# Decay attention and sticky mixture of experts: batch 0's first four heads of q and k turned in fp32 by TensorE, other places in SyncE's queue, another earliest time for gate products

## The chip, the cores and the metric

The kernel runs on one core of one Trainium2 chip. The metric is device time in microseconds (us) of one execution, lower is better. The kernel before takes 856.01 us, the median of 3 runs (855.11 to 859.09).

Engines are named as in the profile: PE (TensorE matmul) and PEld (its weight loads), ACT (ScalarE), DVE (VectorE), POOL (GpSimd), SP (SyncE, which here only issues DMAs, in order). "L868" is line 868 of the kernel before.

## The reference

Attention over 8 batches and 8 heads with 576 positions and a head size of 64, with a decay that is a running sum of logarithms, then a routing of every token to one of 8 experts, which a second gate may keep at the token before.

```python
# q, k, v: 8 x 8 x 576 x 64 fp32, f: 8 x 8 x 576
scores = np.matmul(q, k.transpose(0, 1, 3, 2)) / np.sqrt(D)
cum = np.cumsum(np.log(np.clip(f, 0.0001, 1.0)), axis=-1)
scores = np.where(causal, -1e9, scores + cum[..., :, None] - cum[..., None, :])
attn = softmax(scores)
x = np.matmul(attn, v)                     # tokens: 8 x 576 x 512
logits, local = x @ w_gate, sigmoid(x @ w_local)
# expert of token s: argmax(logits) if s == 0 or local < 0.5, else that of token s - 1
out = p[e] * (np.maximum(x @ w1[e], 0) @ w2[e])   # w1: 8 x 512 x 1024, w2: 8 x 1024 x 512
```

## The kernel before

**Precision.** fp32 numbers are split into two fp16 halves, a high one and the rest, so that matmuls run in fp16. Scores of a head are two matmul passes into one PSUM bank `st`: `Aq` with `Ak` (128 rows: the high and the low half of 64 elements), and `QB` with `KB` (70 rows: the high half again, 64 rows, and 6 rows of decay parts).

**Attention.** A batch is 25 units: per two heads five units of one 512 column bank (c, a, a, b, c), then four units for the last 64 rows (d) and one that joins them. A unit's stages are `sc` (scores on PE, L868, L875), `mx` (row maximum on DVE, L879), `ex` (exponent on ACT, L899, into `P`), `tr` (four fp32 transposes on PE, L914, into `pt`), `hi` and `lo` (the split into `ph` on ACT, L919, and `pl` on DVE, L923) and `av` (the product with v, L893). PSUM holds four banks `st`, two `pt`, two `xp`.

**The planner.** The order on every engine is fixed when the program is built. `issue` (L1221) holds a clock per engine, in ns, with fixed costs per stage, and always issues the stage that could start first by those clocks, with a weight per stage (W, RANK). Extra work is put in by due times (DUE: functions that run once the planned time is reached), by `turns` (PE transposes of the next batch's q and k, L457, with an eviction by ACT or DVE, L466 to L470), by `pump` (POOL's splits), by `ship` (loads on SP), and by a side chain: gate products (`mult`, L816) and the routing steps, mostly DVE operations. A `mult` reads `xt` and `xlt`, which are DMA transposes of the finished tokens `xr` (512 rows) and `xl` (the last 64 rows, L781); `side_next` (L1184) lets it go once the three transposes are issued (`XD`).

**Batch 0's q and k** have a path of their own (`start`, L576). Heads 0 to 3: ACT makes the high half in token layout (`high`, L521), POOL or DVE the low half (`low`), PE turns the halves with two kinds of fp16 matmul (`turn_first`, L546, into `pt`; `turn_high`, L552, into `st`) and adds the decay rows to the second (`add_decay`, L557), DVE and ACT move them to `Aq`, `Ak`, `QB`, `KB` (`untwist`, L561, L563). Heads 4 to 7 are split by POOL (`pieces`, L703 to L705), turned by DMA transposes (`turn`, L362, L365; L370 for the last 64 rows) and copied to QB and KB by DMA. The decay parts come from a chain on ACT and DVE: L228, L229 (logarithm), L231 (scan), then `by_chunks` and `parts` (L238 to L251), which fill `spk`, the operand of `add_decay`. The same `parts` makes `spt` for the last 64 positions.

**SyncE's queue.** SP issues DMAs in program order, and a DMA whose inputs are not ready holds all behind it. The loads of q and k of the batch after next (`load_main`, `load_last`, L162, L169), the copies of the next batch's high halves to QB and KB (`copy_hi`, `copy_last`, L375, L378, L382), the decay rows (L339, L341, L351) and the transposes L751 and L781 all go there. ORD0, ORDA and ORDB (L43 to L45) are lists of moves, two-part codes that `moves` (L621) turns into such issues and POOL steps for batches 0 to 2.

After attention come the experts: matmuls with weights that are loaded and split on the way (L1690, L1712).

Of the kernel before, what the change touches and what calls it, by code (L numbers as in the profile page):

```python
# [9 lines left out]
F32 = mybir.dt.float32  # L10
# [10 lines left out]
BIG = 32768.0  # L21
# [21 lines left out]
ORD0 = moves_of("q:l :k2 q:t4 k:l q:p k:t4 q0:m :sv k:p q:c k:c q1:m q:t k:t :lm q:M k:m :at 0:R 1:R :lv")  # L43
ORDA = moves_of("q0:P k:M 0:V 1:V k:ag")
ORDB = moves_of("q:ag q:G0 2:V q1:P k0:P k1:P q:e k:e 3:V q:G1 k:G0 :vl :Vl q:2 k:G1 :iv v0:P k:2")  # L45
# [20 lines left out]
DUE = (("k2", 11000), ("q2", 12500), ("k3", 14500), ("q3", 15500), ("v", 18000), ("v4", 20500), ("a", 26000), ("b", 29000))  # L66
# [6 lines left out]
def kernel(  # L73
# [38 lines left out]
    nc.gpsimd.memset(ident16, 0.0)  # L112
    nc.gpsimd.affine_select(out=ident16, in_=ident16, pattern=[[-1, 128]], compare_op=ALU.not_equal, fill=1.0, base=0,
                            channel_multiplier=1)
# [37 lines left out]
    mask(mB, 0.0, 2, [[-1, 2], [-2, 64]], 1, ALU.not_equal, BIG)  # L152
    mask(mA, 0.0, 2, [[1, 2], [2, 64]], -1, ALU.is_ge, -BIG)
# [74 lines left out]
    nc.vector.tensor_scalar(ft, ft, 1e-4, 1.0, ALU.max, ALU.min)  # L228
# [125 lines left out]
    def split_qk(b, nm, g0, g1, fast=False):  # L354
        t16, t = Tq[b][nm + "t"], LT[b, nm]
        hi, lo = (t16[:, :, 0:64], t16[:, :, 64:128]) if nm == "q" else (t16[:, :, 64:128], t16[:, :, 0:64])
        split(hi[:, g0:g1], lo[:, g0:g1], t[:, g0:g1], fast)

    def turn(b, nm, h0, h1):
        t16, A = Tq[b][nm + "t"], Tq[b][nm + "A"]  # L360
        if nm == "k":
            nc.sync.dma_start_transpose(out=A[:, 4 * h0:4 * h1], in_=flat(t16[:, 4 * h0:4 * h1]))  # L362
            return
        for c in range(2):
            nc.sync.dma_start_transpose(  # L365
                out=A[:, 16 * c + 2 * h0:16 * c + 2 * h1, :].rearrange("p a (r x) -> p (a r) x", r=2),
                in_=flat(t16[64 * c:64 * c + 64, 4 * h0:4 * h1]))
# [16 lines left out]
    def scale_q(b, g0, g1):  # L384
        t = LT[b, "q"][:, g0:g1]
        nc.scalar.mul(t, t, SCALE)

    def prep_qk(b, nm):

        def begin():  # L390
            new_prep(b, nm)
            prep_aug(b, nm)
            if nm == "q":
                scale_q(b, 0, 16)
                clock["ACT"] += 950

        def turns(h0):
            if nm == "q" and h0 == 0:
                scale_q(b, 16, 36)
                clock["ACT"] += 1150  # L400
            if nm == "k" and h0:
                turn(b, nm, h0, h0 + 5)
            else:
                turn(b, nm, h0, h0 + 4)
                if h0:
                    turn_last(b, nm)

        def half(g0, g1):
            R = {}

            def parts(i):
                t, t16 = LT[b, nm], Tq[b][nm + "t"]
                if not R:
                    hi, lo = (t16[:, :, 0:64], t16[:, :, 64:128]) if nm == "q" else (t16[:, :, 64:128], t16[:, :, 0:64])
                    R["p"] = hi_lo(hi[:, g0:g1], lo[:, g0:g1], t[:, g0:g1], (g1 - g0) // 2)
                R["p"][i][1]()

            return [(64 * (g1 - g0), lambda i=i: parts(i)) for i in range(3)]

        def copy(g0, g1):  # L420
            A, B = Tq[b][nm + "A"], Tq[b][nm + "B"]
            nc.sync.dma_start(out=B[0:64, g0:g1], in_=(A[0:64] if nm == "q" else A[64:128])[:, g0:g1])

        return ([(0, begin)] + half(0, 16) + [(0, lambda: turns(0))] + half(16, 36) + [(0, lambda: turns(4))],
                [(0, lambda: copy(0, 16)), (0, lambda: copy(16, 36))])

    turns = deque()

    def prep_turned(b, nm):
# [20 lines left out]
        def group(j):  # L450
            U = {}

            def tq():
                t16 = Tq[b][nm + "t"]
                U["pt"] = psS.tile([128, 8, 128], F16, name="st")
                for a in range(4 if j == 4 else 8):
                    nc.tensor.transpose(U["pt"][:, a], t16[:, 8 * j + a], ident16)  # L457

            def eq():
# [13 lines left out]
                elif j == 4:  # L473
                    copy_last(b, nm)
# [1792 lines left out]
```

## Time and profile before

| what | value |
|---|---|
| median of 3 runs | 856.01 us (855.11 to 859.09) |
| profiled execution, its own time | 858.83 us |
| its span in the trace | 857.1 us |
| mean granted TensorE clock | 0.976 |
| busy: PE, PEld | 785.4 us (92%), 546.9 us (64%) |
| busy: DVE, ACT, POOL | 529.3 us (62%), 434.4 us (51%), 408.9 us (48%) |

The table is one profiled execution. Busy is the time in which an engine ran something; its idle time is what the views of waits explain. The granted clock is a share of full speed: near 1.0 in a stretch is the level of 2.4 GHz, near 0.5 that of 1.2 GHz. The first score runs at 16 us, batch 1 begins at 70 us, and from about 460 us only experts run.

### The profile page before, as it was taken

The numbers are of one execution on the slowest core, as the hardware profiler recorded it, in microseconds if no ns is written. First come the engines' busy times: TensorE is split into PE (matmuls) and PEld (weight loads), VectorE is DVE, ScalarE is ACT, GpSimd is POOL, SyncE is SP. The second block draws the span as 40 slices with busy tenths as digits, with TensorE's granted clock in tenths as the row PEclk, the third lists the DMA queues.
The fourth block names the chain that finished last, engine by engine and source line by source line (L and its number), as shares of the span: only waits on it lengthen the run. The fifth ranks groups of instructions, "written<-read, shape, count | busy, mean of one in ns | idle before, by whom it ended". The sixth has DMA issues, their size and how long they took to land. (4 is left out here: it accounts for less than half of the span.)

```text
span 857.1 us, 21126 instructions
## 1 busy us (share of the span) xinstructions
PE 785.4 (92%) x8510; PEld 546.9 (64%) x8510; DVE 529.3 (62%) x1125; ACT 434.4 (51%) x807; POOL 408.9 (48%) x479
## 2 busy tenths in 40 slices
PE   5897999889998799878987899999999999999996
PEld 3676778767877678767753555575564847566543
DVE  8885878898867888798848742443163644525120
ACT  4785878758866688657821413333242423324221
POOL 9598938488753968532976252221311212130201
PEclk9998999999989999998999999999999999999999
DMA  7979768596781859329674641848264553736101
GB/s 167 192 165 193 160 112 168 123 180 144 140 197 42 157 140 158 70 47 229 161 165 185 194 142 50 216 147 203 95 171 149 155 182 121 193 116 185 51 0 47
DMA packets 196517, 122.46 MB, mean 143 GB/s; under 512 B 136220, under 2 KB 172318, under 8 KB 196396
## 3 DMA queue, kind: packets, MB, share of 16 engines
q1 hardware_dynamic: 190273, 101.68, 51.6%
q0 software_dynamic: 6144, 19.41, 7.0%
q8 instruction: 68, 1.11, 0.5%
q14 instruction: 32, 0.26, 0.1%
HBM read 72.41 MB, written 19.62 MB: 107 GB/s over the span
## 5 line engine op out<-in xcount | busy, mean ns | idle before, releaser
L1690 PE MATMUL z<-xT,wh 128*128 128x288 f16 (+4 forms) x960 | 182.3, 301 | 3.8 <-DVE hl L1671 3.8
L899 ACT ACTIVATE P<-st,nm 128x512 f32<-128x512 f32 (+3 forms) x288 | 152.4, 584 | 38.5 <-DVE nm L879 35.3
L879 DVE TENSOR_REDUCE nm<-st 128x1 f32<-128x512 f32 (+4 forms) x264 | 134.1, 542 | 23.2 <-PE st L875 16.8
L1671 DVE SCALAR_TENSOR_TENSOR hl<-z,hh 128x576 f16<-128x576 f32 (+5 forms) x80 | 53.0, 662 | 154.0 <-ACT hh L1670 153.8
L919 ACT CAST ph<-pt 128x512 f16<-128x512 f32 (+1 forms) x200 | 115.8, 583 | 50.1 <-PE pt L914 48.6
L914 PE MATMUL pt<-ident,P 128*128 128x128 f32 x784 | 124.7, 283 | 13.0 <-DVE pl L923 8.0
L923 DVE TENSOR_TENSOR pl<-pt,ph 128x512 f16<-128x512 f32 x168 | 111.6, 668 | 26.3 <-ACT ph L919 24.0
L1690 PEld LDWEIGHTS <-wh 128*128 128x128 f16 x960 | 93.2, 98 | 43.7 <-issue 4.9
L1690 PE MATMUL z<-xT,wl 128*128 128x288 f16 (+4 forms) x480 | 118.4, 301 | 0.0
L1712 PE MATMUL y<-uh,hh 128*128 128x512 f16 x288 | 109.9, 381 | 1.6 <-ACT o L1680 1.6
L1712 PE MATMUL y<-uh,hl 128*128 128x512 f16 x288 | 109.9, 382 | 0.0
L1712 PE MATMUL y<-ul,hh 128*128 128x512 f16 x288 | 109.7, 381 | 0.0
L1670 ACT ACTIVATE hh<-z 128x576 f16<-128x576 f32 (+5 forms) x80 | 46.0, 575 | 121.1 <-PE z L1690 121.0
L914 PEld LDWEIGHTS pt<-ident,P 128*128 128x128 f32 x784 | 85.8, 144 | 28.9 <-issue 7.5
L1712 PEld LDWEIGHTS <-hh 128*128 128x128 f16 x576 | 56.5, 98 | 70.4 <-issue 6.2
L1682 POOL DMA_INDIRECT out_dram<-o,ranki x26 | 27.3, 1051 | 149.0 <-ACT o L1680 115.8
L893 PE MATMUL xp<-VH,pl 128*128 128x65 f16 (+1 forms) x960 | 92.3, 195 | 4.3 <-DVE pl L923 4.3
L893 PE MATMUL xp<-VH,ph 128*128 128x65 f16 (+1 forms) x960 | 94.3, 198 | 0.9 <-ACT ph L919 0.9
L893 PE MATMUL xp<-VL,ph 128*128 128x65 f16 (+1 forms) x960 | 93.2, 196 | 0.0
L893 PEld LDWEIGHTS <-ph 128*128 128x128 f16 (+1 forms) x1920 | 85.0, 103 | 7.7 <-issue 2.5
L868 PE MATMUL st<-KB,QB 70*128 70x256 f16 (+4 forms) x448 | 80.1, 287 | 8.5 <-DMA KB<-Ak 7.1
L868 PE MATMUL st<-Ak,Aq 128*128 128x256 f16 (+4 forms) x448 | 80.7, 291 | 7.3 <-ACT P L899 7.1
(390 smaller groups left out, 1316.3 us busy)
## 6 DMA issues: line engine op xcount, KB each, us to landing
stg<-in_moe_w_dram SPq DMA_DIRECT2D x64, 512.0 KB
xs<-xr SPq DMA_DIRECT2D x16, 512.0 KB
ldq<-in_q_dram SPq DMA_DIRECT2D x14, 512.0 KB
ldk<-in_k_dram SPq DMA_DIRECT2D x14, 512.0 KB
ldv<-in_v_dram SPq DMA_DIRECT2D x28, 256.0 KB
QB<-Aq SPq DMA_DIRECT2D x15, 256.0 KB
KB<-Ak SPq DMA_DIRECT2D x15, 256.0 KB
ldv<-in_v_dram SPq DMA_DIRECT2D x20, 64.0 KB
```

The lines of the kernel that those rows point to most:

```text
L868: nc.tensor.matmul(st[p0:p0 + m, co:co + n], lhsT=queries(lq, kk, h, c), rhs=rhs, start=(ps == 0 and first and co == col), stop=(ps == 1), ...
L879: nc.vector.tensor_reduce(dst, src, axis=AX.X, op=ALU.max, negate=True)
L893: nc.tensor.matmul(xo, lhsT=a[:, c0:c0 + m], rhs=w[:, vi, :], start=False, stop=(i == n - 1 and jj == 2), skip_group_check=True)
L899: nc.scalar.activation(P[:, c0:c1].rearrange("p (k x r) -> p k r x", r=2, x=64), st[:, c0:c1].rearrange("p (k r x) -> p k r x", r=2, x=64) ...
L914: nc.tensor.matmul(U["pt"][:, i * 128:(i + 1) * 128], lhsT=P[:, i * 128:(i + 1) * 128], rhs=ident, is_transpose=True, start=(i == 0), stop ...
L919: nc.scalar.copy(U["ph"][:, :cols], U["pt"][:, :cols])
L923: nc.vector.tensor_tensor(U["pl"][:, :cols], U["pt"][:, :cols], U["ph"][:, :cols], ALU.subtract)
L1670: nc.scalar.activation(hv, z[:, 0:nh, 0:wd], AF.Relu)
L1671: nc.vector.scalar_tensor_tensor(lv, z[:, 0:nh, 0:wd], 0.0, hv, ALU.max, ALU.subtract)
L1682: nc.gpsimd.indirect_dma_start(out=outf, out_offset=bass.IndirectOffsetOnAxis(ap=scat(t), axis=0), in_=o, in_offset=None, bounds_check=NT ...
L1690: nc.tensor.matmul(z[:, a, 0:wd], lhsT=w[:, d, fc * 128:(fc + 1) * 128], rhs=xT[:, x, a * wd:(a + 1) * wd], start=(i == 0), stop=(i == len ...
L1712: nc.tensor.matmul(y, lhsT=a[:, fc, t * 128:(t + 1) * 128], rhs=u[:, fc], start=(i == 0), stop=(i == len(prods) - 1))
```

## The change

Batch 0's heads 0 to 3 are turned by PE in fp32, straight from the loaded q and k, each head's four blocks into one bank (`turn_head`); after `add_decay` ACT reads the bank twice, for the high half in Aq or Ak (`head_hi`) and for QB or KB (`head_b`), and DVE makes the low half from the bank and the high half (`head_lo`). Heads 4 to 7 and the last 64 rows are still split by POOL, and are then turned by PE as in later batches (`group`, the former inner function of `prep_turned`), with evictions by ACT or DVE; the DMA transposes of q and k are gone. The planner gets these turns as entries with a ready time (LATE), and batch 0's later units need them. The factor on q moves into the evictions; the decay constants in `pick` make up for it.

Of the small work, `spk` and KB's ones are set by DVE and QB's by ACT (one ACT table load more); `spt` is made by POOL (`last_parts`); v's heads 2 to 7 of batch 0 are split by POOL, where ACT and DVE took heads 2 to 5; some masks come later. In SP's queue the loads of q and k for heads 4 to 7 stand ahead of v and of the decay parts, and the lists ORD0 to ORDC put batch 0's to 2's loads and copies in another order. A `mult` may not start by the planner before `XR`, 4.5 us behind the issue of the last rows' transpose.

```diff
-ORDB = moves_of("q:ag q:G0 2:V q1:P k0:P k1:P q:e k:e 3:V q:G1 k:G0 :vl :Vl q:2 k:G1 :iv v0:P k:2")
+ORDB = moves_of("q:ag q:G0 2:V q1:P k0:P k1:P 3:V q:G1 k:G0 :vl :Vl k:G1 :iv v0:P")
+ORDC = moves_of("q:2"), moves_of("k:2")
...
+XL = 4500
+LATE = ((12500, 'kh'), (13500, 'qh'), (15500, 'q2'), (15500, 'q3'), (17500, 'k2'), (17500, 'k3'), (22000, 'q4'), (23000, 'k4'))
...
+    for c in range(2):
+        nc.scalar.activation(flat(QB[0][64:70, 16 * c + 8:16 * c + 16]), ident[64:70, 0:1].broadcast_to([6, 1024]), AF.Copy,
+                             scale=0.0, bias=-1.0)
...
+    def turn_head(h, nm):
+
+        st = psX.tile([128, 512], F32, name="xp") if h == 2 else psS.tile([128, 512], F32, name="st")
         for a in range(4):
+            nc.tensor.matmul(st[0:64, 128 * a:128 * a + 128], lhsT=LT[0, nm][:, 4 * h + a], rhs=ident, is_transpose=True,
                              start=(a == 0), stop=True, skip_group_check=True)
         return st
...
+    def head_hi(st, h, nm):
+        nc.scalar.activation(of_head(Tq[0][nm + "A"], TOP if nm == "q" else LOW, h, nm), of_bank(st, 64, nm), AF.Copy,
+                             scale=SCALE if nm == "q" else 1.0)
+
+    def head_b(st, h, nm):
+        nc.scalar.activation(of_head(Tq[0][nm + "B"], slice(0, 70), h, nm), of_bank(st, 70, nm), AF.Copy,
+                             scale=SCALE if nm == "q" else 1.0)
...
+        for h in range(2):
+            heads(h)
+            for nm in "kq":
+                head_hi(HS[h, nm], h, nm)
+        decays(0)
+        decays(1)
+        heads(2)
+        decays(2)
+        for h in range(2):
+            for nm in "kq":
+                head_b(HS[h, nm], h, nm)
+                head_lo(HS[h, nm], h, nm)
         load_v(0, groups=((2, 8),), last=False)
+        vh, vl, v0 = parts_v(0, 2)
+        nc.scalar.copy(vh, v0)
+        for x in pieces("q", 4, 8):
+            x()
+        nc.gpsimd.tensor_tensor(vl, v0, vh, ALU.subtract)
...
             XD[b] = XD.get(b, 0) + 1
+            XR[b] = max(clock["POOL"], clock["PE"]) + XL
...
+        if hasattr(chain[0], "batch") and side["run"] is None:
+            after.append((XR[chain[0].batch], "PE"))
```

On SP, at the end of batch 0, the copies of batch 1's high halves (QB_121 and KB_123 before, QB_109 and KB_111 now, both from Aq and Ak) and the loads of batch 2's q and k stand like this. Before:

```order
L182 DMA ldv<-in_v_dram 128x8x64
L185 DMA ldv<-in_v_dram 64x4x64 x2
L162 DMA ldq<-in_q_dram 128x8x128 x2
L169 DMA ldq<-in_q_dram 64x4x64 x2
L162 DMA ldk<-in_k_dram 128x8x128 x2
L169 DMA ldk<-in_k_dram 64x4x64 x2
L378 DMA QB_121<-Aq 64x2x1024 x2
L382 DMA QB_121<-Aq 64x512
L375 DMA KB_123<-Ak 64x2048 x2
L382 DMA KB_123<-Ak 64x512
```

Now:

```order
L185 DMA ldv<-in_v_dram 64x4x64 x2
L362 DMA QB_109<-Aq 64x2x1024 x2
L366 DMA QB_109<-Aq 64x512
L162 DMA ldq<-in_q_dram 128x8x128 x2
L169 DMA ldq<-in_q_dram 64x4x64 x2
L359 DMA KB_111<-Ak 64x2048 x2
L366 DMA KB_111<-Ak 64x512
L162 DMA ldk<-in_k_dram 128x8x128 x2
L169 DMA ldk<-in_k_dram 64x4x64 x2
```

The copies to QB moved ahead of both loads, those to KB ahead of the load of k.

On SP, in batch 4, the transpose of batch 3's last rows (xlt) and the copies for batch 5, before:

```order
L757 DMA xs<-xr 64x4x1024 x2
L378 DMA QB_121<-Aq 64x2x1024 x2
L382 DMA QB_121<-Aq 64x512
L339 DMA KB_123<-augm 3x4096
L351 DMA KB_123<-augt 3x512
L781 DMA_TRANSPOSE xlt<-xl 128x4x128
L787 DMA xs<-xl 128x1x256 x2
```

Now:

```order
L732 DMA xs<-xr 64x4x1024 x2
L756 DMA_TRANSPOSE xlt<-xl 128x4x128
L763 DMA xs<-xl 128x1x256 x2
L362 DMA QB_109<-Aq 64x2x1024 x2
L366 DMA QB_109<-Aq 64x512
L341 DMA KB_111<-augm 3x4096
L353 DMA KB_111<-augt 3x512
```

The transpose moved ahead of four DMA groups; the same holds two batches later.

On DVE, at the third block of routing steps (HI, RH, LO), at the end of batch 6, before:

```order
L1473 TENSOR_TENSOR hm<-t_192,ov 128x10
L1479 TENSOR_TENSOR HI<-imain,hm 128x480
L1483 TENSOR_SCALAR RH<-HI,irow 128x10x48
L1485 TENSOR_SCALAR RH<-HI,irow 128x2x48
L1490 TENSOR_TENSOR RH<-HI,icol 128x10x48
L1491 TENSOR_TENSOR LO<-i_176,lo 128x1280
L879 TENSOR_REDUCE nm<-st 128x1 x5
```

Now:

```order
L855 TENSOR_REDUCE nm<-st 128x1 x2
L1451 TENSOR_TENSOR hm<-t_188,ov 128x10
L855 TENSOR_REDUCE nm<-st 128x1 x2
L1457 TENSOR_TENSOR HI<-imain,hm 128x480
L855 TENSOR_REDUCE nm<-st 128x2
L1461 TENSOR_SCALAR RH<-HI,irow 128x10x48
L899 TENSOR_TENSOR pl<-pt,ph 128x512
L1463 TENSOR_SCALAR RH<-HI,irow 128x2x48
L855 TENSOR_REDUCE nm<-st 128x1
L1468 TENSOR_TENSOR RH<-HI,icol 128x10x48
L1469 TENSOR_TENSOR LO<-i_172,lo 128x1280
```

The row maxima of the units that follow stand among the steps now, where they stood behind them.

## Rows read from the trace of the kernel before

**Rows 1.** What PE waited for, whole span (us in total, times, longest us).

```profile
PE st L868 <- DMA KB<-Ak: 7.1, 3, 4.5
PE st L868 <- ACT P L899: 7.1, 6, 4.7
PE st L816 <- DMA xlt<-xl: 4.4, 2, 2.4
PE st L868 <- DMA KB<-augt: 1.4, 1, 1.4
```

**Rows 2.** Busy time by engine in stretches around PE's long waits (stretch, its length, then each engine's busy us with its instructions, the granted TensorE clock, the DMA share and GB/s).

```profile
24.90:28.50 3.60, 3.60 (x20) 2.41 (x19) 1.77 (x4) 1.81 (x4) 1.69 (x2) 0.53 0.79 124
28.50:70.30 41.80, 38.02 (x590) 31.36 (x588) 35.09 (x74) 35.83 (x73) 33.39 (x44) 1.00 0.91 197
...
74.80:79.90 5.10, 5.10 (x73) 4.09 (x73) 2.89 (x6) 2.44 (x5) 3.17 (x3) 0.54 0.88 80
...
246.70:253.60 6.90, 6.86 (x43) 5.41 (x44) 3.44 (x11) 2.65 (x6) 0.68 (x2) 0.51 0.91 219
...
353.20:355.90 2.70, 2.70 (x19) 1.73 (x17) 2.13 (x7) 0.86 (x2) 2.45 (x5) 0.50 0.00 0
...
387.90:394.50 6.60, 6.58 (x48) 4.75 (x48) 4.46 (x14) 4.91 (x11) 0.00 (x0) 0.58 1.04 265
```

**Rows 3.** The end of batch 0 in order of time (start, length, engine, line, what, count, idle time before it and what ended it): SP's issues, and PE's second score pass of batch 1.

```profile
60.32 1.84 SPq L162 DMA_DIRECT2D ldk<-in_k_dram  x2
...
64.52 1.32 SPq L378 DMA_DIRECT2D QB<-Aq  x2
...
66.67 2.68 SPq L375 DMA_DIRECT2D KB<-Ak  x2
...
74.80 0.59 PE L868 MATMUL st<-KB,QB 70*128 70x512 f16 x1 [4.53 <-DMA KB<-Ak]
```

**Rows 4.** Size of one DMA of the loads of k (count, KB each), from the list of DMA issues up to 75 us, and the DMA rate (last column) in two stretches of the view by stretches.

```profile
ldk<-in_k_dram SPq DMA_DIRECT2D x4, 512.0 KB
...
60.00:65.00 5.00, 5.00 (x88) 4.32 (x87) 4.97 (x10) 4.06 (x10) 4.83 (x6) 1.00 1.19 274
...
70.00:75.00 5.00, 0.47 (x3) 0.20 (x2) 0.92 (x2) 0.37 (x1) 4.83 (x6) 0.76 1.17 184
```

**Rows 5.** The gate product of batch 3 in order of time: POOL's split of the last rows, SP's queue, and PE's wait; the last row is the same wait two batches later.

```profile
237.41 0.67 POOL L314 TENSOR_TENSOR xl<-xnl,xl 128x256 f16<-128x256 f32 x1
239.91 1.76 SPq L378 DMA_DIRECT2D QB<-Aq  x2
243.77 1.83 SPq L781 DMA_TRANSPOSE xlt<-xl  x1
246.74 0.59 PE L816 MATMUL st<-wg,xlt 128*64 128x18 f16 x8 [1.94 <-DMA xlt<-xl]
351.26 0.42 PE L816 MATMUL st<-wg,xlt 128*64 128x18 f16 x8 [2.42 <-DMA xlt<-xl]
```

**Rows 6.** The third block of routing steps in order of time: its last step on DVE, the row maxima behind it, and PE.

```profile
385.05 1.48 DVE L1491 TENSOR_TENSOR LO<-i,lo 128x1280 f16<-128x1280 f16 x1
386.45 3.32 DVE L879 TENSOR_REDUCE nm<-st 128x1 f32<-128x512 f32 x7
387.92 0.59 PE L868 MATMUL st<-Ak,Aq 128*128 128x512 f16 x1 [4.66 <-ACT P L899]
```

**Rows 7.** The start in order of time, all engines.

```profile
5.01 0.68 ACT L229 ACTIVATE lg<-ft 64x576 f32<-64x576 f32 x1 [2.93 <-DVE ft L228]
5.71 1.28 ACT L230 ACT_TABLE_LOAD   x1
7.00 0.20 ACT L230 ACTIVATE one<-one 1x1 f32<-1x1 f32 x1
11.30 0.78 DVE L246 CAST spk<-lg 4x512 f16<-4x512 f32 x1
12.13 1.01 PE L557 MATMUL st<-spk,pick 97*6 97x512 f16 x2 [0.74 <-DVE spk L246]
15.98 0.61 PE L868 MATMUL st<-Ak,Aq 128*128 128x512 f16 x1
16.57 2.20 POOL L705 TENSOR_TENSOR t16q<-ldq,t16q 128x1024 f16<-128x1024 f32 x1
16.82 2.00 DVE L247 CAST spt<-cu 64x64 f16<-64x64 f32 x1
18.66 0.41 PE L552 MATMUL st<-ident,t16k 128*64 128x128 f16 x4
21.41 0.38 PE L552 MATMUL st<-ident,t16k 128*64 128x128 f16 x4 [0.34 <-ACT QB L563]
24.28 0.38 PE L546 MATMUL pt<-ident,t16k 128*128 128x128 f16 x4 [2.17 <-DVE Ak L561]
26.93 1.06 PE L914 MATMUL pt<-ident,P 128*128 128x128 f32 x4
```

**Rows 8.** Durations up to 75 us by line and shape (count, busy us, mean ns), and a run of transposes from the view in order of time, at the full clock.

```profile
L466 ACT ACTIVATE Ak<-st 128x1024 f16<-128x1024 f16 x3 | 3.1, 1078 | 0.0
L563 ACT CAST QB<-st 70x512 f16<-70x512 f32 x4 | 2.3, 582 | 1.9 <-PE st L557 1.9
...
64.12 1.91 PE L457 MATMUL st<-ident,t16k 128*128 128x128 f16 x28
```

More of the change, by code (lines that the diff above doesn't have):

```diff
@@ L382, in copy_last @@
         nc.sync.dma_start(out=B[0:64, 32:36], in_=(A[0:64] if nm == "q" else A[64:128])[:, 32:36])
[L384 to L402, printed above, removed]
-            else:
[L404 to L425, printed above, removed]
@@ L513, in prep, with last_parts @@
         return q + [mark("q")] + k + [mark("k")] + v + last
+    def last_parts():
+        x = cu[:, 512:576]
+        for j in range(3):
+            nc.gpsimd.tensor_scalar(spt[:, j], x, 1.0, 1.0, ALU.mult, ALU.mult)
+            if j < 2:
+                nc.gpsimd.tensor_tensor(x, x, spt[:, j], ALU.subtract)
     def put_aug():
@@ L611, in start, with due_1, due_2 @@
         for x in ORD0:
+            moves(x)
+    def due_1():
+        assert all(n > -9 or u['key'][2] > 1 for n, u, _ in line['tq'])
+        for x in ORD1:
+            moves(x)
+    def due_2():
+        for x in ORD2:
             moves(x)
@@ L676, in moves @@
             u, i = b
[L677 to L683 removed]
+            for y in prep_v(1) if u == "v" else halves(1, u, *((0, 16), (16, 36))[int(i)]):
+                y[1]()
         else:
@@ L693, in due_b @@
     def due_b():
+        assert all(n > -9 for n, u, _ in line['tq'])
         for x in ORDB:
@@ L696, in due_b, with due_c @@
         open_small()
+        EX["run"] = True
+    def due_c(i):
+        for x in ORDC[i]:
+            moves(x)
     def pieces(nm, h0, h1):
@@ L730, in split_v, with decays @@
-    def split_v(h0, h1, fast=False):
-        tv = [x.rearrange("p (c h) d -> p c h d", c=4) for x in (VH[0][:, 0:32], VL[0][:, 0:32], LT[0, "v"][:, 0:32])]
-        split(tv[0][:, :, h0:h1, 0:64], tv[1][:, :, h0:h1, 0:64], tv[2][:, :, h0:h1], fast)
-    def due_v(h0, h1):
-        split_v(h0, h1, True)
-        clock["ACT"] += 480
-        clock["DVE"] += 600
-    XT, XD = {}, {}
+        for nm in "kq":
+            HS[h, nm] = turn_head(h, nm)
+    def decays(h):
+        for nm in "kq":
+            add_decay(HS[h, nm], h, nm)
@@ new lines, in due_head, with head_3, tq, eq @@
+    def due_head(nm):
+        head_hi(HS[2, nm], 2, nm)
+        head_b(HS[2, nm], 2, nm)
+        head_lo(HS[2, nm], 2, nm)
+        clock["ACT"] += 960
+        clock["DVE"] = max(clock["DVE"] + 640, clock["ACT"] + 800)
+    def head_3(nm):
+        U = {}
+        def tq():
+            U["st"] = turn_head(3, nm)
+            add_decay(U["st"], 3, nm)
+        def eq():
+            for f in head_hi, head_b, head_lo:
+                f(U["st"], 3, nm)
+            clock["DVE"] = max(clock["DVE"], clock["ACT"] + 1100) + 640
+        return {"key": (0, nm, -1), "tq": ("PE", 500, tq, {"psS": 1}, {}), "eq": ("ACT", 960, eq, {}, {"psS": 1})}
@@ L1773 @@
                 init_gate()
-            if not due:
+            if "run" in EX:
                 if b < B - 1 or i < XP:
```

251 lines of the change are left out of this document (97 added, 154 removed).

## Prediction

> **What bounds the kernel now.** I read PE's waits first, then busy time and granted clock around the long ones, then SP's queue and the start in order of time. PE is busy for 92% of the span, so time is to be had only where PE waits, or where it runs at the slow clock afterwards. The list of waits [rows 1] has four long single waits that this change can reach: 4.53 us for KB at the end of batch 0, 1.94 and 2.42 us for the last rows' transpose (xlt) in batches 4 and 6, and 4.66 us for a free bank at the end of batch 6. Behind each, the granted clock is near one half [rows 2]: 0.54 for 5.10 us, 0.51 for 6.90, 0.50 for 2.70, 0.58 for 6.60. PE is busy throughout these stretches, so a stretch of length t at clock c costs t x (1 - c): 2.3, 3.4, 1.35 and 2.8 us. The reader is to see that a wait costs about as much again behind it. From 460 us on only experts run, and nothing there is touched; a gain in attention is a gain at the end, since engine orders are fixed and serial.
>
> **The change part by part.** The sum is made against the profiled execution's own 858.83 us, which is 2.8 us above the median of 856.01.
>
> *End of batch 0.* The copies to KB are issued from 66.67 us, and PE gets the first one's data at 74.80 [rows 3]. They are 64 KB to 256 KB; what makes them late is what stands ahead in the queue: the loads of batch 2's q and k, of which those of k went out from 60.32. Two of these are 512 KB each, so k alone has 1.05 MB; at the rates of 274 and 184 GB/s of these microseconds [rows 4] that is 3.8 to 5.7 us of transfer. The order now has the KB copies ahead of the load of k, and the QB copies ahead of both loads. A transfer 3.8 to 5.7 us sooner covers a wait of 4.53, so I take it as gone, with the 2.3 us of slow clock: 6.8 us. Bounds: 0 (the load of q, still ahead, is enough to be late) to 6.8.
>
> *The gate products in batches 4 and 6.* POOL's split of the last rows is done at 238.08 (237.41 + 0.67), but SP issues the transpose at 243.77, because the QB copies of the next batch stand ahead, and these wait for evictions until 239.91 [rows 5]. PE then waits until 246.74. In the new order the transpose stands ahead of those copies in both batches, so it can go out some 5 us sooner, more than either wait. The products themselves stay at nearly the same place in PE's order. I take both waits and the slow stretches behind: 1.94 + 3.4 + 2.42 + 1.35 = 9.1 us. Bounds: 0 to 9.1. In batch 2 it is the other way round: the transpose now stands behind the copies, but the product comes some five units later, which is more than the 5 us lost.
>
> *End of batch 6.* DVE does the routing steps in one block to 386.53, and only then the seven row maxima for which ACT's exponents, and by them PE's banks, wait [rows 6]: 4.66 us and 2.8 behind. Now maxima stand between the steps. This comes out of the planner's arithmetic, not of an edit to the route, and DVE's work is the same; so I take half, 3.7 us, bounds 0 to 7.5.
>
> *The start.* (a) ACT has one more table load and two QB fills ahead of the logarithm. A load is 1.28 us [rows 7], a fill of 1024 columns about the 1.08 of the nearest row [rows 8]; together 3.4 us. ACT idles 2.93 us ahead of the logarithm, so 0.5 is left over: `spk` is complete at 12.08 + 0.5 = 12.6. (b) PE then has four decay products (two take 1.01), eight fp32 turns of head 2 (four fp32 transposes take 1.06 at this clock) and two decay products more before the first score: 2.0 + 2.1 + 1.0 = 5.1, so 17.7 instead of 15.98: 1.7 later. The turns of heads 0 and 1 need only loaded q and k and lie under the decay chain. (c) Head 2's turning, 18.66 to 21.41 before, is then behind: 2.75 back. (d) The 2.17 us for which PE waits at 24.28 are DVE's: its casts for `spt` lie beside POOL's long operations (16.82 for 2.00, POOL from 16.57 for 2.20). They are on POOL now, so that wait goes, and with it the slow stretch up to 28.5 at 0.53, 3.60 x 0.47 = 1.7 [rows 2]. (e) PE gets 40 fp16 turns of heads 4 to 7 and the last rows, which DMA did: 28 take 1.91 [rows 8], so 2.7 us. Head 3's turns are about equal. Sum: +1.7 - 2.75 - 2.17 - 1.7 + 2.7 = -2.2. Bounds: a chain whose cast meets a long POOL operation is held by up to 2.20 - 0.78 = 1.4, and without the gains of (d) this is +3.1 + 2.7 - 2.75 = +3.1; with the turns at the full clock (b) is half as long, and it is -4.8.
>
> The Trainium skill (ScalarE: Activation LUTs, "What ACT_TABLE_LOAD costs") gives 1283 ns for a load and about 1380 ns of drain, 2.66 us for a switch. The trace agrees with the first number only: the load ends at 6.99 and the next activation starts at 7.00 [rows 7]. By the page the logarithm, and all behind it, would be another 1.4 us later and the forecast 843.0; by the row nothing is added, and I go by the row.
>
> *What hides the rest.* New evictions (three of up to 1.08 on ACT, the others on DVE, one ACT cast of 0.58 more per head and operand) lie beside PE from 28.5 to 70.3, where ACT is busy 35.83 of 41.80 us and DVE 35.09 [rows 2]; two v casts leave ACT and three subtractions DVE. That cover is some 6 us; if it were gone, ACT's part is 2 x 1.08 + 0.6 + 4 x 0.58 less two v casts of about 0.6, near 4 us. The wait of 1.4 for the last rows' decay parts of KB [rows 1] goes, since their DMAs stand ahead of batch 1's v now: 1.4, bounds 0 to 1.4.
>
> *What the new order brings elsewhere.* Every later batch is planned anew, and waits like the four can arise where there were none. On average one of the four costs (4.53 + 1.94 + 2.42 + 4.66) / 4 = 3.4 and 2.5 behind, 5.9 us. I take one and a half of them, +8.8; bounds 0 and three, 17.7.
>
> Sum: -6.8 - 9.1 - 3.7 - 2.2 - 1.4 + 8.8 = -14.4: 844.4 for an execution like the profiled one, 841.6 for the median.
>
> **The rivals.** *The waits move.* The gate and routing terms (12.8 us) come back in other places and one more of 5.9 with them instead of one and a half: -10.4 + 5.9 = -4.5, 851.5. For it: these four waits are accidents of an order that the planner made with fixed costs, and it makes a new one with the same costs. Against it: the transposes of the last rows have moved for good, and the planner now counts 4.5 us for them.
>
> *The copies to KB stay late.* The load of q, as large as that of k, still stands ahead, and the evictions of k come last; the 6.8 do not come: 848.4. Against it: 1.05 MB less are ahead.
>
> *POOL is late in batch 0 (slower).* Place: the turns of the last rows of k, which stand in PE's order ahead of the second wave of scores. POOL has three splits of v more ahead of them (half of a 2.20 operation and its copy, some 1.7 us each, an estimate from [rows 7], so 5 us) and v's loads stand behind the decay parts in SP's queue. If POOL splits the last rows 5 us after PE is there, PE waits 5 and runs slow behind it for 2.5: with the waits moved as in the first rival, +7.5 - 4.5 = +3.0, and with ACT's cover gone as well +7.0, 863 for the median. It decides when PE's wait there passes some 12 us, or 5 where the gate terms fail too. Against it: POOL drops the low halves of heads 0 to 3 and q's scaling.
>
> *It does not do what it says.* The start may gain nothing, as the first score comes no sooner (17.7); with +3.1 for the start it is 846.9.
>
> **How the numbers follow.** Forecast 58%, own range 833 to 849; waits moved 17%; KB late 10%; start without gain 9%; slower 6%. Half a per cent, about what a measurement of this kernel tells from no change, is 4.3 us: faster means below 851.7. Of the waits moved, half lies below it; all of the forecast, KB late and the start count as faster but for 2 points: 58 + 10 + 9 + 8 - 2 = 83%. Same: 9 + 2 = 11%; slower 6%. The range of 8 in 10 is 830 to 853: below 830 all terms come at nearly their upper bounds with no new wait (-23.2), above 853 are the upper half of the waits moved and the slower case.
>
> **What would show it.** First score near 17.7 us and no wait of PE near 24; the wait for KB at the end of batch 0 below 1 us and the granted clock near 1.0 in the 5 us behind it; no wait of PE for xlt above 0.5 us; the first maxima of batch 7 before the last routing step. The prediction is wrong if the KB wait is still 4 us, if PE's waits in batches 2 to 7 have not fallen in sum, or if batch 1 begins later than the 70 us of now.

## The result and the profile after

The changed kernel takes 834.2 us, the median of 4 runs (832.92 to 835.73), against 856.55 for the kernel before on the same chip: ratio 0.9737, 95% interval 0.9705 to 0.9769, or 22.4 us less where 14.4 were forecast. The profiled execution takes 835.73 us, its span is 834.0.

To see where the gain lies, both spans are cut at the same three points of PE's work: the first mask product of the last rows' unit (L974 before, L950 after) of batches 0, 1 and 7. The first stage holds the start and most of batch 0, the second the step to batch 1, the third batches 2 to 6 with what overlaps them, the fourth the rest and the experts. The view of windows, kernel before (columns as in [rows 2]):

```profile
0.00:55.30 55.30, 39.54 (x458) 29.84 (x458) 46.23 (x83) 36.98 (x72) 43.94 (x70) 0.97 0.79 168
55.30:106.60 51.30, 45.01 (x699) 36.92 (x695) 37.90 (x80) 35.56 (x72) 46.21 (x79) 0.93 0.90 183
106.60:413.97 307.37, 278.22 (x4439) 226.56 (x4434) 252.96 (x604) 225.37 (x461) 192.06 (x211) 0.96 0.66 137
413.97:857.10 443.13, 422.63 (x2931) 253.59 (x2926) 192.25 (x359) 136.48 (x205) 126.66 (x122) 0.99 0.48 139
sum 857.10, PE 785.41 PEld 546.92 DVE 529.35 ACT 434.39 POOL 408.87; mean PE 196.35 PEld 136.73 DVE 132.34 ACT 108.60 POOL 102.22
```

The same view of the kernel after:

```profile
0.00:54.04 54.04, 42.58 (x519) 33.87 (x519) 42.45 (x89) 45.38 (x83) 39.04 (x69) 0.97 0.67 154
54.04:97.55 43.51, 40.38 (x650) 32.77 (x646) 35.44 (x75) 33.71 (x68) 41.69 (x51) 1.00 0.92 183
97.55:389.56 292.01, 269.63 (x4434) 221.75 (x4430) 252.73 (x604) 224.10 (x461) 197.54 (x240) 0.99 0.69 147
389.56:834.00 444.44, 424.12 (x2930) 254.09 (x2926) 193.49 (x359) 136.70 (x205) 126.55 (x121) 0.99 0.49 139
sum 834.00, PE 776.71 PEld 542.48 DVE 524.11 ACT 439.90 POOL 404.82; mean PE 194.18 PEld 135.62 DVE 131.03 ACT 109.97 POOL 101.20
```

The stages change by -1.26, -7.79, -15.36 and +1.31, in sum -23.1 us. PE's busy time falls by 8.7 us, but times the mean granted clock it is 785.41 x 0.976 = 767 before and 776.71 x 0.989 = 768 after. So PE's work is nearly the same, and the gain is 14.4 us of idle time and 8.7 us of slow clock.

PE's waits after (us in total, times, longest), against [rows 1]:

```profile
PE pt L890 <- DVE pl L899: 12.1, 15, 1.9
...
PE xp L869 <- DVE pl L899: 5.4, 7, 2.3
...
PE st L844 <- ACT P L875: 3.9, 9, 0.7
...
PE st L844 <- DMA KB<-Ak: 0.2, 1, 0.2
```

No wait for xlt is left, that for KB is 0.2 us in place of 7.1, and the one of 4.66 us of a score for a free bank has no successor above 0.7. The longest wait in batches 1 to 7 is 2.3 us.

The start after, in order of time on ACT, DVE and PE (answers to [rows 7]):

```profile
4.11 1.28 ACT L231 ACT_TABLE_LOAD   x1
5.40 0.68 ACT L231 ACTIVATE lg<-ft 64x576 f32<-64x576 f32 x1
...
6.32 1.06 PE L478 MATMUL st<-ident,ldq 128*64 128x128 f32 x4
...
9.46 0.28 DVE L251 COPY spk<-spm 4x512 f16<-4x512 f16 x1
9.76 0.68 DVE L253 TENSOR_TENSOR lg<-lg,spm 64x512 f32<-64x512 f32 x1
10.48 0.42 DVE L248 CAST spk<-lg 4x512 f16<-4x512 f32 x1
...
11.04 1.02 PE L483 MATMUL st<-spk,pick 97*6 97x512 f16 x4 [1.95 <-DVE spk L248]
11.99 0.63 PE L478 MATMUL xp<-ident,ldk 128*64 128x128 f32 x4
...
12.99 0.59 PE L483 MATMUL xp<-spk,pick 97*6 97x512 f16 x2
13.58 0.39 PE L844 MATMUL st<-Ak,Aq 128*128 128x512 f16 x1
```

The first score starts at 13.58 us, earlier than before (15.98) and not later, as forecast (17.7). The logarithm starts at 5.40, 0.39 later than before, as forecast; but the chain from there to `spk` is faster (its last cast takes 0.42 in place of 0.78), and PE is at full speed already: four decay products in 1.02 us, where two took 1.01. This is read from durations (four fp32 turns take 1.06 us at 6.32 and 0.63 at 11.99); the view of windows gives a granted clock of 1.00 for all of 5.50 to 13.58, and before for 8.96 to 15.98.

The gate product of batch 3, in order of time on POOL, SP and PE (answers to [rows 5]):

```profile
216.71 0.67 POOL L316 TENSOR_TENSOR xl<-xnl,xl 128x256 f16<-128x256 f32 x1
222.28 3.25 SPq L756 DMA_TRANSPOSE xlt<-xl  x1
...
228.54 0.42 PE L792 MATMUL st<-wg,xlt 128*64 128x18 f16 x8
```

The transpose stands ahead of the QB copies now, but it still goes out 4.9 us after POOL is done (217.38): SP is busy with issues of its own until then. What has moved is the product, 6.26 us behind the issue of the transpose, where it was 2.97.

### The profile page after: what moved, and what is told of

It reads as the page before. It is cut to its first block, busy times and chain, and to the rows that moved or that the text cites. A ratio compares the mean times of both kernels' runs of the same rounds, so it can differ in the third digit from the quotient of the medians.

```text
span 834.0 us, 21130 instructions
## 1 busy us (share of the span) xinstructions
PE 776.7 (93%) x8518; PEld 542.5 (65%) x8518; DVE 524.1 (63%) x1125; ACT 439.9 (53%) x814; POOL 404.8 (49%) x478
## 4 chain that ended last, share of the span: by engine, by line
PE 58%; DVE 14%; issue 9%; DMA 7%; ACT 5%; POOL 4%; POOLq 1%; SPq 1%; ACTq 0%; DVEq 0%
PE z L1668 15%; PE y L1690 13%; PE pt L890 8%; PE st L844 7%; PE xp L869 6%; DVE nm L855 3%; PE st L382 2%; DVE pl L899 2%; DMA xT<-xg 2%; ACT P L875 1%; POOLq L1659 1%; DMA out_dram<-o,xs 1%; ACT ph L895 1%; DMA stg<-in_moe_w_dram 1%; PE y L1694 1%
## 5 line engine op out<-in xcount | busy, mean ns | idle before, releaser
L890 PE MATMUL pt<-ident,P 128*128 128x128 f32 x784 | 121.8, 280 | 16.3 <-DVE pl L899 12.1
L844 PE MATMUL st<-Ak,Aq 128*128 128x256 f16 (+4 forms) x448 | 77.2, 283 | 3.9 <-ACT P L875 3.9
L869 PEld LDWEIGHTS <-pl 128*128 128x128 f16 (+1 forms) x960 | 75.4, 103 | 6.4 <-DVE pl L899 6.2
```

The source lines that it names most:

```text
L844: nc.tensor.matmul(st[p0:p0 + m, co:co + n], lhsT=queries(lq, kk, h, c), rhs=rhs, start=(ps == 0 and first and co == col), stop=(ps == 1), ...
L869: nc.tensor.matmul(xo, lhsT=a[:, c0:c0 + m], rhs=w[:, vi, :], start=False, stop=(i == n - 1 and jj == 2), skip_group_check=True)
L890: nc.tensor.matmul(U["pt"][:, i * 128:(i + 1) * 128], lhsT=P[:, i * 128:(i + 1) * 128], rhs=ident, is_transpose=True, start=(i == 0), stop ...
```

## The experiments

Two edits come apart cleanly: the place of batch 2's loads ("loads"), and the earliest time of gate products ("guard"). Each was undone in the kernel after and made alone in the kernel before. What is left is the start with batch 0's turns.

**Loads put back in the kernel after.**

```diff
-ORDB = moves_of("q:ag q:G0 2:V q1:P k0:P k1:P 3:V q:G1 k:G0 :vl :Vl k:G1 :iv v0:P")
+ORDB = moves_of("q:ag q:G0 2:V q1:P k0:P k1:P 3:V q:G1 k:G0 :vl :Vl q:2 k:G1 :iv v0:P k:2")
-DUE = (('k2', 11500), ('q2', 12300), ('0', 12500), ('1', 20600), ('2', 25000), ('a', 27000), ('b', 29000), ('c0', 47000), ('c1', 56000))
+DUE = (('k2', 11500), ('q2', 12300), ('0', 12500), ('1', 20600), ('2', 25000), ('a', 27000), ('b', 29000))
```

> The kernel after, with the loads of batch 2's q and k put back ahead of batch 1's copies to QB and KB in SyncE's queue; the order of every other engine is unchanged. Theory (these loads alone made the KB copies late, and late copies are paid at once): PE waits 3.5 to 4.5 us for KB at the start of batch 1 where it waits 0.2 now, about 2 us of slow clock follow, 839 to 841 us against 834.2. Rival (the copies come early because the start and the evictions have moved, and the queue has slack): the wait stays under 1 us, 834 to 835. Second rival (a late start of batch 1 is absorbed by later waits): the wait comes, but the time moves by less than 2 us.

Ratio 0.982 (0.976 to 0.988), 0.8% or 7.1 us worse than after. PE is at batch 1 as early as in the kernel after, and waits there:

```profile
66.56 0.38 PE L844 MATMUL st<-Ak,Aq 128*128 128x512 f16 x1
74.01 0.59 PE L844 MATMUL st<-KB,QB 70*128 70x512 f16 x1 [7.07 <-DMA KB<-Ak]
...
53.23:106.80 53.57, 43.23 (x651) 34.71 (x645) 35.95 (x75) 33.75 (x68) 46.53 (x81) 0.90 0.86 180
```

The wait is longer than expected, because PE arrives earlier (66.94 against 70.27 before) while KB comes at almost the same time (74.01 against 74.80). The first theory holds: the wait comes with the loads, and the time with it. When exactly KB comes differs from one execution to another: the kernel with the start alone, below, has the same order on SP and PE up to here, and in its trace KB came at 72.17.

**Loads moved in the kernel before.**

```diff
-ORDB = moves_of("q:ag q:G0 2:V q1:P k0:P k1:P q:e k:e 3:V q:G1 k:G0 :vl :Vl q:2 k:G1 :iv v0:P k:2")
+ORDB = moves_of("q:ag q:G0 2:V q1:P k0:P k1:P q:e k:e 3:V q:G1 k:G0 :vl :Vl k:G1 :iv v0:P")
+ORDC = moves_of("q:2"), moves_of("k:2")
...
```

The two lists run at 47000 and 56000 of the planner's clock, as in the kernel after; what waited for the last due time there (splits, loads and turns of later batches) still starts with ORDB's.

> The kernel before, with only the loads of batch 2's q and k moved behind batch 1's copies to KB (q behind part of the QB copies, k far behind); PE, ACT, DVE and POOL keep their order. Theory: the 4.53 us wait at 70.27 goes and with it 2.3 us of slow clock: 849 to 851 us against 856.5. Rival (the late copies are followed by a second bound, such as the loads that now come late themselves): PE's wait only changes its name, 854 to 857.

Ratio 0.9954 (0.992 to 0.998): 3.9 us less by the ratio, of 6.8 forecast. The spans of the profiled executions differ by more, 849.6 against 857.1, but that execution is 2.3 us below its kernel's median, and that of before is above its own. The wait at 70 us is gone, and the second stage falls from 51.30 to 45.80. The rest of the kernel keeps its waits.

```profile
67.58 3.28 SPq L376 DMA_DIRECT2D KB<-Ak  x2
...
71.64 0.38 PE L874 MATMUL st<-KB,QB 70*128 70x512 f16 x1
```

The copies to KB are issued no sooner here than before (67.58 against 66.67), yet their data is there by 71.64 where it came at 74.80. So what the loads cost is their transfer ahead of the copies, as the forecast reckoned, and not a later issue.

**Guard taken out of the kernel after.**

```diff
         if hasattr(chain[0], "batch") and side["run"] is None:
-            after.append((XR[chain[0].batch], "PE"))
+            pass
```

> The kernel after without the earliest time XR for gate products; everything is planned anew. Theory (the transposes of the last rows stand earlier in the queue now, and the guard adds to it): xlt waits of PE come back in part, 2 to 4 us in sum, 835 to 839 us. Rival A (the guard alone removed the waits): 4 to 9 us come back, 838 to 843. Rival B (the place in the queue alone did it): no xlt wait above 0.5 us, 832.5 to 836, the spread of a new plan.

Ratio 0.9902 (0.987 to 0.993), 14 us worse than after, more than any of the three expected. The waits, the product of batch 3 and the block at the end of batch 6, from three views:

```profile
PE st L792 <- DMA xlt<-xl: 6.9, 3, 3.4
...
234.82 1.54 SPq L756 DMA_TRANSPOSE xlt<-xl  x1
237.66 0.42 PE L792 MATMUL st<-wg,xlt 128*64 128x18 f16 x8 [1.73 <-DMA xlt<-xl]
...
375.91 3.32 DVE L855 TENSOR_REDUCE nm<-st 128x1 f32<-128x512 f32 x7
377.38 0.58 PE L844 MATMUL st<-Ak,Aq 128*128 128x512 f16 x1 [3.61 <-ACT P L875]
...
97.57:403.27 305.70, 277.19 (x4436) 225.52 (x4430) 253.00 (x604) 225.48 (x461) 195.25 (x238) 0.96 0.66 140
```

Without the guard the third stage is 305.70 us, as before (307.37), with the waits for xlt, the wait for a bank at the end of batch 6 and the slow clock (0.96) of the kernel before. The product of batch 3 stands 2.84 us behind the issue again. DVE's block of routing steps is whole again too, with seven maxima behind its last step, as in [rows 6]. So the guard brings the routing term too, which the forecast had counted at half because no edit aimed at it.

**Guard alone in the kernel before.**

```diff
-    XT, XD = {}, {}
+    XT, XD, XR = {}, {}, {}
...
             XD[b] = XD.get(b, 0) + 1
+            XR[b] = max(clock["POOL"], clock["PE"]) + 4500
...
+        if hasattr(chain[0], "batch") and side["run"] is None:
+            after.append((XR[chain[0].batch], "PE"))
```

> The kernel before with only the earliest time for gate products added (4.5 us behind the planned issue of the last rows' transpose); planned anew from batch 2 on. Rival A (the guard alone removed the waits): no xlt wait, up to 9.1 us less, 847 to 850 against 856.5. Theory (part guard, part queue): one of the two waits of 1.94 and 2.42 stays in part, 850 to 854. Rival B (queue alone): both stay, 855 to 858.

Ratio 0.9896 (0.987 to 0.993): 8.9 us less. The third stage falls by 16.8 us to 290.61, but the fourth grows by 6.0, where PE now waits for the last gate's transposes:

```profile
243.95 1.21 SPq L781 DMA_TRANSPOSE xlt<-xl  x1
...
252.18 0.42 PE L817 MATMUL st<-wg,xlt 128*64 128x18 f16 x8
...
430.04 0.60 PE L817 MATMUL psG<-wg,xt 128*128 128x18 f16 x16 [5.02 <-DMA xt<-xr]
...
106.79:397.40 290.61, 271.62 (x4451) 222.92 (x4446) 248.09 (x604) 225.12 (x462) 187.18 (x213) 0.98 0.68 140
```

This is a new wait of the size that the forecast charged for. The first two lines are the gate product of batch 3: its transpose still goes out behind the QB copies, 5.7 us after POOL's split as in the kernel before, but the product stands 8.23 us behind it and no wait for xlt is left. So the place in the queue is not what takes the wait away; and in the kernel after without its guard the QB copies stand ahead of the transpose again, so that place comes with the guard too.

**Both in the kernel before.**

> The kernel before with the guard and with the loads of batch 2's q and k behind batch 1's KB copies: both parts that lie behind batch 0, without the new start. The guard alone gave 0.9896, the loads alone 0.9954. Theory (they add, the loads being worth 4.0 us of wait and 1.9 of slow clock in the run with the guard): 0.982 to 0.986; what is left to after's 0.974 is the start and the 5.0 us wait for xt near 425 us that the guard alone brought. Rival (one hides the other): 0.988 to 0.990.

0.985 (0.981 to 0.989): they add. From here to after it is 1.1%: the start with its turns, and the 4.0 us wait for xt that this kernel also has. Its profile has a wait of 4.9 us besides, for a copy to KB in batch 0 (up to 35.63), which no other kernel with the start of before shows there.

**The start alone** (kernel after, guard and loads both undone).

> The kernel after without the guard and with the loads of batch 2's q and k ahead of batch 1's copies: of the change, what is left is the start, batch 0's turns and the queue ahead of them. Theory (batch 1 can't begin before the KB copies have landed, and these come behind loads that the new start doesn't move): the start's 3.3 us end in that wait, which is 6 to 8 us long in place of 4.5; ratio 0.995 to 1.002. Rival (the parts add: 0.974 + 0.008 + 0.016): 0.998 as well if they add, but with the KB wait unchanged at 4 to 5 us and batch 1's last rows 2 to 3 us earlier than in the kernel before (106.6 us).

1.0002 (0.998 to 1.002): nothing of the start is left in the time.

```profile
72.17 0.58 PE L844 MATMUL st<-KB,QB 70*128 70x512 f16 x1 [5.64 <-DMA KB<-Ak]
```

The time fits the theory and the rival alike, and the signs that were to tell them apart do not: the wait of 5.64 us lies between the two, and the last rows of batch 1 come at 104.28, 2.3 us sooner than before, as the rival has it. PE is ready for batch 1 at 66.52, 3.7 us sooner than before, and the longer wait takes 1.1 of that back; with the loads put back in the kernel after, where the wait was 7.07, the last rows of batch 1 came at 106.81. Then waits like those of before follow (xlt three times, 4.76 for a bank). The spans of the profiled executions still differ by 2.1 us (855.0 and 857.1), the medians of 10 and 13 runs by nothing, so where the start's gain is lost can't be read from these traces.

| | guard and loads of before | loads moved | guard | both |
|---|---|---|---|---|
| start of before | 1 | 0.9954 | 0.9896 | 0.985 |
| start of after | 1.0002 | 0.9902 | 0.982 | 0.9737 |

The parts don't simply add: the start is worth nothing by itself, and 0.5% to 1.1% with the others, each of these differences being known to some 0.5%.

**Is the order after a lucky one?** Three other plans with a guard: 2.0 us and 6.0 us in place of 4.5, and one planner cost changed.

```diff
-XL = 4500
+XL = 2000
```

> The kernel after with the earliest time of gate products 2.0 us behind the planned issue of the last rows' transpose in place of 4.5. Without it altogether three xlt waits of 1.81, 1.73 and 3.38 us stood, and the ratio to before was 0.990 where after has 0.974. Theory (the guard works by keeping PE from the transpose's latency, and the later waits grow from such stalls): with 2.0 us PE still comes 1 to 3 us early in some batch; xlt waits of 1 to 4 us in sum and a ratio of 0.977 to 0.985. Rival (any guard only happens to give another plan): no xlt wait and 0.972 to 0.977, or as late as without it, 0.99.

0.9733 (0.969 to 0.977), no xlt wait. My theory was wrong in this: the guard need not be as long as the transpose takes. In the trace of this kernel every product stands 5.3 us or more behind the issue of its transpose, as in the kernel after (6.3 or more). The ten products that made PE wait (two before, two with the loads alone, three without the guard, three with the start alone) stood 2.5 to 3.5 behind it. The 2.0 us are counted on the planner's clock, the 5.3 in the trace.

```diff
-XL = 4500
+XL = 6000
```

> The kernel after with the earliest time of gate products 6.0 us behind the issue in place of 4.5; a sixth of PE's rows stand in another order. Theory (a guard as long as the latency or longer does it, whatever the exact plan): no xlt wait, ratio 0.970 to 0.978. Rival (the plan of after is a lucky one and another is worth what the forecast charged for new waits): 0.980 to 0.990.

0.9741 (0.970 to 0.978), no xlt wait.

```diff
-    COSTS = {"mult": ("PE", 1100), "half": ("ACT", 116), "add": ("DVE", 200), "rows": ("PE", 200), "rows2": ("ACT", 260),
+    COSTS = {"mult": ("PE", 1100), "half": ("ACT", 116), "add": ("DVE", 230), "rows": ("PE", 200), "rows2": ("ACT", 260),
```

> The kernel after with one planner cost changed (a gate's addition on DVE 230 ns in place of 200), which changes no work and keeps the guard, but puts a fifth of PE's rows in another order. It shows what a new plan by itself costs. Theory (the long waits are gone with the guard): ratio 0.970 to 0.980, no PE wait above 2.5 us between batches 1 and 7. Rival (lucky plan; one and a half waits of 5.9 us with their slow clock come somewhere): 0.982 to 0.992.

0.9717 (0.966 to 0.977); the longest PE wait between batches 1 and 7 is 1.8 us. The plan is not a lucky one: with a guard, five plans of the new start (these three, the order of after, and the one below) have a third stage of 286 to 301 us; without a guard, four kernels with either start have 305.7 to 307.8.

**A better known cost.**

```diff
-                u["lo"] = "DVE", 70 + 1.04 * cols, lo, {"pl": 1}, {"psT": 1}
+                u["lo"] = "DVE", 70 + 1.17 * cols, lo, {"pl": 1}, {"psT": 1}
```

> The kernel after with the planner's cost of a low half on DVE at 1.17 ns per column in place of 1.04 (669 ns for 512 columns; the profile of after shows 670): no work changes, a sixth of PE's rows move. PE's waits for low halves are the largest group left in attention, 12.1 + 5.4 us. Theory (a planner that knows the duration leaves fewer such waits): 12 us in sum or less, and 0.966 to 0.972. Rival (they come from the depth of the chain, not from that cost): the spread of a new plan, 0.970 to 0.978.

0.9805 (0.975 to 0.987), a miss on both theories: the waits for low halves do fall, from 17.5 to 12.1 us (8.3 and 3.8), but the kernel is slower than after, by 0.7%, with intervals that just overlap. The third stage is the 301 us of the range above:

```profile
98.40:399.00 300.60, 279.35 (x4511) 229.00 (x4505) 252.26 (x605) 228.15 (x468) 205.65 (x244) 0.97 0.66 141
```

Its granted clock is 0.97 where after has 0.99. So a new plan with a guard can cost some us; why this one does was not tried further.

**POOL busy beside the decay chain.** No other engine's order changes; `dum` and `du2` are new tiles of 512 columns, fp16 and fp32, that nobody reads.

```diff
-    spk = cp.tile([97, 512], F16, name="spk")
+    spk, dum, du2 = cp.tile([97, 512], F16, name="spk"), cp.tile([128, 512], F16, name="dum"), cp.tile([128, 512], F32, name="du2")
...
-        other_masks()
+        other_masks(); nc.gpsimd.memset(dum, 0.0); nc.gpsimd.memset(du2, 0.0); [nc.gpsimd.tensor_tensor(dum, du2, dum, ALU.subtract) for _ in range(5)]
```

> The kernel after with five subtractions of 128x512 and two fills on GpSimd that nobody reads, put where GpSimd idles from 4.8 to 11.1 us beside the decay chain; no other engine's order changes. Theory (the chain on DVE was slower before because GpSimd worked beside it): copies of 0.28 us take 0.5 to 0.65, the casts of 0.42 up to 0.78, the subtraction of 0.68 about 1.06; the last part of spk ends 0.8 to 1.5 us later than at 10.90 and the first score starts 0.8 to 1.5 us later than at 13.58; the time grows by 0 to 1.5 us, ratio 0.973 to 0.976. Rival (the difference came from the order of the chain or from what ACT and PE did): spk within 0.3 us of 10.90.

The direction held, the size was far off. POOL and DVE in this kernel:

```profile
5.77 7.80 POOL L529 TENSOR_TENSOR dum<-du,dum 128x512 f16<-128x512 f32 x5
...
11.30 1.26 DVE L249 CAST spm<-lg 64x512 f16<-64x512 f32 x1
12.59 1.12 DVE L251 COPY spk<-spm 4x512 f16<-4x512 f16 x1
13.55 1.07 POOL L664 TENSOR_SCALAR t16q<-ldq 128x1024 f16<-128x1024 f32 x1
13.73 1.43 DVE L253 TENSOR_TENSOR lg<-lg,spm 64x512 f32<-64x512 f32 x1
14.70 2.43 POOL L665 TENSOR_TENSOR t16q<-ldq,t16q 128x1024 f16<-128x1024 f32 x1
15.19 2.23 DVE L248 CAST spk<-lg 4x512 f16<-4x512 f32 x1
```

`spk` is complete at 17.42 in place of 10.90, 6.5 us later. Of these, 4.0 are there when the copy ends (13.71 against 9.74), beside the added subtractions, which end at 13.57. The other 2.5 come behind them: POOL's split of q, which in the kernel after begins at 11.12, when the chain is over, now lies beside the chain's last two steps. The last rows' unit of batch 0 comes 7.5 us later (61.51 against 54.04), that of batch 1 7.9, and the ratio is 0.984 (0.979 to 0.989), 1.0% or 8.8 us worse than after. So a microsecond of the start is about one at the end, as far as that interval (some 4.5 us to either side) tells, once the copies to KB no longer set when batch 1 begins.

**A shorter start.** The kernel with the changed cost of a gate's addition, and QB's two fills on POOL while it idles:

```diff
     for c in range(2):
-        nc.scalar.activation(flat(QB[0][64:70, 16 * c + 8:16 * c + 16]), ident[64:70, 0:1].broadcast_to([6, 1024]), AF.Copy,
-                             scale=0.0, bias=-1.0)
+        pass
...
         mask(minus, 0.0, 1, [[0, 1], [-1, 128]], 1, ALU.not_equal, -1.0)
+        for c in range(2):
+            nc.gpsimd.memset(QB[0][64:70, 16 * c + 8:16 * c + 16], -1.0)
```

> The kernel after with the planner's cost of a gate's addition at 230 ns (the run with that alone gave 0.9717) and with the two fills of QB's rows moved from ACT to GpSimd, which idles from 4.8 us on; so one ACT table load goes too. The logarithm started at 5.40 although its input was ready at 4.61. Theory (the start is serial, and a microsecond of it is one at the end, as the run with a busy GpSimd showed): the logarithm starts at 4.6 to 4.7, spk is complete 0.6 to 0.8 us sooner, at 10.1 to 10.3, and the time falls by as much: ratio 0.968 to 0.973. Rival (the fills on GpSimd slow DVE's scan and casts as its subtractions did, or PE's turns are not done by then): spk at 10.6 or later and 0.971 to 0.976.

0.9695 (0.967 to 0.972), the lowest of all; its interval still overlaps those of after and of the changed cost alone (0.9717), so the time does not show what the fills are worth. The start does what the theory said:

```profile
4.63 0.68 ACT L230 ACTIVATE lg<-ft 64x576 f32<-64x576 f32 x1 [2.55 <-DVE ft L229]
...
9.71 0.42 DVE L247 CAST spk<-lg 4x512 f16<-4x512 f32 x1
...
12.81 0.39 PE L845 MATMUL st<-Ak,Aq 128*128 128x512 f16 x1
```

The logarithm and the first score both come 0.77 us sooner than after.

## Why the prediction was right in sign and too small

*End of batch 0, -6.8.* Right. PE begins batch 1 with a wait of 0.21 us in place of 4.53 and at a granted clock of 1.00. Undoing the edit costs 7.1 us, with a wait of 7.07. In the kernel before, where the wait is 4.53, the same edit is worth 3.9 (1.4 to 6.5); the two intervals overlap. The rival of a late KB fell: the load of q still stands ahead, and the wait is gone.

*The start and the wait for augt, -2.2 and -1.4.* The sum was right: with the loads put back PE stops for KB at 66.94 where it was 70.27 before, 3.3 us against 3.6. The steps in it were not, so that the sum agrees is luck. (a) Of the logarithm's 0.5, 0.39 came, but `spk` is complete at 10.90 and not at 12.6, since the trace of before had the chain beside a busy POOL; I had read that contention in (d) for `spt` and not here. The run with POOL busy shows that POOL's work alone can stretch this chain. (b) From `spk` to the first score it is 2.68 us and not 5.1, because I priced the products and turns at the slow speed; PE works from 5.50 on now, where it began at 8.96, and its durations are those of full speed from 11.04. (d) The wait near 24 is gone, but one of 1.35 at 25.39 is new, and a stretch at half clock stays: 0.51 from 20.04 to 23.39, where it was 24.9 to 28.5. (e) The turns came as counted: up to the first score of batch 1 PE does 112 fp16 turns (L382), where it did 72 (L457). That the first stage ends only 1.26 us sooner, with a first score 2.40 us sooner, does not price them, since 28 turns of batch 1 have moved into it, 1.9 us by [rows 8]. On the table load trace and forecast agree: the logarithm starts 0.01 us after the load, with no drain between them.

*The gate products, -9.1.* The waits went, but not for the reason given. "It can go out some 5 us sooner" was wrong: the transpose of batch 3 still goes out 4.9 us after POOL's end (5.7 before). Without the guard the xlt waits are back, 6.9 us in sum, with the loads' place unchanged; with the guard alone they are gone, with the transpose's place in the queue unchanged. The forecast named the guard only as an argument against a rival.

*The routing block, -3.7 of 7.5.* All of it went. I took half because it looked like the planner's luck; the runs show that it goes with the guard. Without a guard there is a wait of 3.6 to 4.8 us at the end of batch 6 (before, no guard, loads alone, start alone); in the kernels with one none of that kind is above 1.7.

*New waits elsewhere, +8.8.* This is the step that failed. Together the last three terms were -4.0; the third and fourth stage give -15.36 + 1.31 = -14.05, close to the named terms at full size, -9.1 - 7.5 = -16.6, so by this difference new waits are worth about +2.5, not +8.8. The order of after and three other plans with the new start and a guard have none above 2.3 us in batches 1 to 7; what grew is PE's group of short waits for low halves (12.3 to 17.5 us). The charge was not absurd: the guard in the kernel before brought a wait of 5.0 us near its end, and the changed cost of low halves a slow third stage. But I priced four waits as four accidents of which new ones would arise, and three of them go with one edit. What the guard has to be is loose (2.0 and 6.0 us do as well as 4.5); that there is one decides. The last step to the wait at the end of batch 6 shows in the traces: without the guard DVE does the routing steps as one block again, ahead of seven maxima. How an early gate product makes the planner put them so, 30 us later, was not traced, and whether the plans without it could be mended in another way wasn't tried. All terms but the charge come to -23.2, which the forecast calls nearly their upper bounds; these are -29.6, and -23.2 from the median is 832.8, not below 830. It is what came (-23.1 between the profiled executions), the first two stages 1.4 us short of their terms and the others 1.3 above theirs.

*The rivals.* Waits that only move did not come. POOL was not late for the last rows of k: no wait of PE in batch 0 behind the start is above 1.35. Of the signs to watch, the first score was wrong (13.58 for 17.7), the others came: no xlt wait, KB below 1 us, batch 1 before 70 us (66.99), PE's idle time in the third stage down from 29.2 to 22.4 us, and DVE's maxima between the routing steps:

```profile
363.12 0.33 DVE L1461 TENSOR_SCALAR RH<-HI,irow 128x480 f16<-128x480 f16 x1
...
364.26 0.68 DVE L855 TENSOR_REDUCE nm<-st 128x1 f32<-128x512 f32 x1
364.86 0.65 DVE L1468 TENSOR_TENSOR RH<-HI,icol 128x480 f16<-128x480 f16 x1
```

## What to carry to other kernels

Where a fixed order comes from a planner with fixed costs, look for the latency that it doesn't know, and give it that one: several waits in different places can be one missing latency, and they then go together. A gain ahead of a wait on a transfer can be worth nothing until the transfer comes sooner too; test such parts in both orders, not one alone. Read durations in a start chain only together with what runs beside it.

## What was not expected of the hardware

DVE and POOL slow each other far more than forecast. Beside the five added subtractions, which took 1.56 us each (7.80 / 5) where one of that shape takes 1.12 in the kernel after, DVE's cast of 0.42 us took 1.26 and its copy of 0.28 took 1.12. Beside POOL's split of q, which follows them, the subtraction of 0.68 took 1.43 and the last cast, of 0.42, took 2.23; the split's second operation took 2.43 itself, 2.13 in the kernel after. The Trainium skill (SBUF — State Buffer, "Who interferes with whom") says that VectorE and GpSimd share a pair of ports, and that, when VectorE is in one of its two-port modes, whichever instruction issues first keeps that pair to its end while the other is blocked. The trace agrees in the times, though no run here shows the mode: the cast of 2.23 us began 0.49 us behind the split's operation and ended at 17.42, 0.29 us behind that operation's end at 17.13. The 1.94 us that were left of it and the cast's own 0.42 are more than 2.23, so one such block is enough for it.

A wait of PE is not always followed by the slow clock. After two of the longest in attention, 1.91 us up to 265.30 and 2.26 up to 277.30, the windows show a granted clock of 0.66 and of 1.00:

```profile
265.30:270.30 5.00, 5.00 (x50) 4.14 (x51) 4.05 (x7) 1.44 (x3) 4.82 (x6) 0.66 0.98 173
277.30:282.30 5.00, 4.79 (x78) 4.13 (x79) 4.01 (x9) 3.96 (x8) 4.60 (x8) 1.00 0.48 122
```

The forecast put the slow stretch behind each wait on the bill as a rule; it is worth that for the four long waits of before, not for every wait.
